# A list scheduler's DMA rate: 310 GB/s in place of 360 in the plan of a fused long-convolution and MLP kernel

## The chip, the cores and the metric

The kernel runs on one core of a Trainium2 chip. The metric is device microseconds for one execution. The kernel before takes 866.74 us, the median of three runs (866.11 to 869.25).

The core has five instruction streams that matter here: TensorE (matmuls; PE in the profile, its weight loads PEld), VectorE (DVE), ScalarE (ACT), GpSimd (POOL, here nearly only issuing accumulating transfers) and SyncE (SP, which only issues transfers). Each works through its own queue in program order and waits for the others on semaphores.

## The reference: what is computed

Two kinds of layers alternate on a sequence of 2048 rows of 640 channels, each behind a layer norm and with a residual: A gates the normed rows with a long causal convolution, B is an MLP with a hidden width of 1728. The weights and the operands of A are the same both times.

```python
def _A_ref(q, k, v, shift_k, ssm_k, ssm_D):
    ...  # k_shift: causal depthwise convolution of k with 4 taps
    kv = k_shift * v
    ...  # y: causal depthwise convolution of kv with ssm_k, 2048 taps, by FFT
    y = y + kv * ssm_D[None, None, :]
    return q * y

def _B_ref(x, w1, w2):
    h = jnp.maximum(jnp.einsum("bsd,df->bsf", x, w1), 0)
    return jnp.einsum("bsf,fd->bsd", h, w2)

x = A_q
x = x + _A_ref(_layernorm(x), A_k, A_v, A_shift_k, A_ssm_k, A_ssm_D)
x = x + _B_ref(_layernorm(x), B_w1, B_w2)
x = x + _A_ref(_layernorm(x), A_k, A_v, A_shift_k, A_ssm_k, A_ssm_D)
x = x + _B_ref(_layernorm(x), B_w1, B_w2)
```

## The kernel before

**Tiling.** The 2048 rows are cut into 8 chunks of 256, each of two halves of 128 rows; the 640 channels into 5 tiles of 128. The convolution does not depend on x, so its result (Y, kept in DRAM) is made once and used by both A layers. It is done chunk by chunk in a transformed domain: `transform` loads a unit (one or two tiles of a chunk: kt, vt, hf, hr), applies the four taps (ACT L381 and DVE L412 or L418, product with v at L419, sums at L421 and L422, filter sums gs at L403), and transforms signal and filter with matmuls against constant matrices (pg L435, L458; pt L481; pr L498; split in three matmuls at L315 to L317) into A and G tiles of 128x768 (results moved at L438, L462 to L464, L473, L508, L511). `spills` writes these to DRAM (L528, L529), and `products` reads them again for all later chunks (Ax, Gx at L566), multiplies and sums them on VectorE (L575, L578, L579), and transforms back (pq at L601 or L315 to L317, ys at L633 and L634, stored at L642).

**The MLP.** `norms` loads all weights (ws, L674), squares them on TensorE (pw, L681) for a scale (L686 to L697, pn at L688), and `wsplit` makes two half-precision parts of each (ScalarE L708, VectorE L709). `prep` makes the layer input of a chunk: norm, gate with Y, residual, norm (L765 to L786, L827, L831), and splits it in two half-precision parts (xh at ACT L860 and DVE L861; in the first chunk at L840 to L845). These are transposed by transposing transfers (L873) or, for the very first 128 rows, by TensorE (xt, L880, copied out at L884 and L886). `main` multiplies with w1 (h and hb, L994, L996, L1006, L1007, L1009), splits the activations into a high part hh (ScalarE, L1045) and a low part hl (VectorE, L1046), with special lines for the last narrow block (tb L1049, L1058, L1050, L1051, L1059, L1060), and multiplies with w2 (o and oc, L978, L979, L981). The residual goes in at L1136. The last three MLP layers take another form of the second product (L933).

**What sets the order.** All of this is recorded as operations of a `Plan`: engine, estimated cost, tiles read and written, priority, and for transfers the bytes. `Plan.order` runs a list schedule over a modelled clock: whenever an engine is free, it takes the ready operation of the best priority whose output tiles have room. The order found is then issued and fixed; on the chip no engine departs from it. Three places use the modelled transfer:

- An operation with `nbytes` set moves a variable `dma`, the time at which the modelled transfer path is free: it starts from the later of its old value and now plus 1.9 us, and grows by bytes over a rate. The tiles written become ready 1.1 us later (L201 to L204).
- SyncE takes nothing while `dma` lies more than `LAG` (3 us) ahead of now (the lines at the start of the loop over engines). In that time operations of better priority may become ready and go first.
- Everything that reads a loaded tile becomes ready after it, and so the order of TensorE, VectorE and ScalarE follows too.

Priorities (`CLS`): urgent steps of the MLP first, then loads for it (SOON), the convolution of the first chunks (CONV), spills (SPILL), the convolution of later chunks (LATER), and MLP matmuls as filler (FILL). Rings of buffers (`Ring`) bound how far work can run ahead: 4 buffers each for Ax and Gx together and for A and G, one each for kt, vt, hf, hr.

Of the kernel before, what the change touches and what calls it, by code (L numbers as in the profile page):

```python
# [45 lines left out]
CRIT, SLACK = -1, 0.6  # L46
PEOUT = 0.35
SAFE = 1.5
LATE_DOWN = 0.0


def LATE(o):
    return SAFE if o.prio[0] in CLS[3:5] else o.late

# [39 lines left out]
class Plan:  # L94
# [33 lines left out]
    def order(self):  # L128
        engs = sorted({o.eng for o in self.ops})
        free = dict.fromkeys(engs, 0.0)  # L130
        cand = {e: [] for e in engs}
        soon = {e: [o for o in self.ops if o.eng == e and o.prio[0] == CRIT] for e in engs if e != "SP"}
        for o in self.ops:
            if not o.left:
                cand[o.eng].append(o)
        events, dma, n, out = [0.0], 0.0, 0, []

        def fits(o):
            at = {}
            for t in o.new:  # L140
                k = at.setdefault(t.ring, {})
                if sum(k.values()) >= t.ring.free or t.ring.lines[t.stream][k.get(t.stream, 0)] is not t:
                    return False
                k[t.stream] = k.get(t.stream, 0) + 1
            return True

        finish, later = [], []
        now = 0.0
        while n < len(self.ops):
            if not events:  # L150
                stuck = [(o.eng, o.seq, [t.name for t in o.new]) for e in engs for o in cand[e]]
                raise RuntimeError(f"no order: {stuck[:12]}")
            now = heapq.heappop(events)
            while events and events[0] <= now:
                heapq.heappop(events)
            while finish and finish[0][0] <= now:
                _, _, o = heapq.heappop(finish)
                for t in o.tiles:
                    t.left -= 1
                    if not t.left and t.ring is not None:  # L160
                        t.ring.free += 1
                for d in o.outs:
                    if d.eng == "PE" != o.eng and LATE(d):
                        heapq.heappush(later, (now + LATE(d), d.seq, d))
                        heapq.heappush(events, now + LATE(d))
                        continue
                    if d.eng == "PE" == o.eng:
                        continue
                    d.left -= 1
                    if not d.left:  # L170
                        cand[d.eng].append(d)
            while later and later[0][0] <= now:
                _, _, d = heapq.heappop(later)
                d.left -= 1
                if not d.left:
                    cand["PE"].append(d)
            for e in engs:
                if free[e] > now + 1e-9:
                    continue
                if e == "SP" and dma > now + LAG:  # L180
                    heapq.heappush(events, dma - LAG)
                    continue
                best = None
                rooms = [(max(d.ready for d in o.deps) - now + SLACK, o.prio) for o in soon.get(e, ()) if o.left and all(d.start is not None for d in o.deps)]
                for o in cand[e]:
                    if best is not None and o.prio > best.prio:
                        continue
                    if any(o.cost > room and o.prio > prio for room, prio in rooms):
                        continue
                    if fits(o):  # L190
                        best = o
                if best is None:
                    continue
                cand[e].remove(best)
                for t in best.new:
                    t.ring.free -= 1
                    t.ring.lines[t.stream].pop(0)
                best.start = now
                free[e] = now + best.cost
                end = free[e] + (PEOUT if e == "PE" else 0.08)  # L200
                if best.nbytes:  # L201
                    dma = max(dma, now + 1.9) + best.nbytes / 360e3
                    end = dma + 1.1
                best.ready = end  # L204
                if best.prio[0] == CRIT and e in soon:
                    soon[e].remove(best)
                if e == "PE":
                    for d in best.outs:
                        if d.eng == e:
                            d.left -= 1  # L210
                            if not d.left:
                                cand[e].append(d)
                heapq.heappush(finish, (end, best.seq, best))
                heapq.heappush(events, end)
                heapq.heappush(events, free[e])
                out.append(best)
                n += 1
        return out, now
# [11 lines left out]
def tile_h3_mlp(ctx: ExitStack, tc: tile.TileContext, q, kT, vT, shk, hF, hR, dD, w1, w2, cM, cG, out):  # L230
# [21 lines left out]
    def pe(cost, fn, reads, writes, prio, late=0.0):  # L252
        plan.op("PE", cost, fn, reads, writes, prio, late=late)

    def act(n, fn, reads, writes, prio, extra=0.0):
        plan.op("ACT", 0.1 + n * 0.00083 + extra, fn, reads, writes, prio)
# [632 lines left out]
    def main(n, a, layer, S, xTS):  # L889
# [130 lines left out]
        for j in JS:  # L1020
# [36 lines left out]
            if j == NFP - 1:  # L1057
                pe(0.0545 * len(S), lambda p1=p1: PE.matmul(p1[:, 0:R], down.t, tb[:, 0:R], start=False, stop=True, skip_group_check=True), [tb, down], [p1], URGENT, LATE_DOWN * len(S) / 2)  # L1058
                act(R, lambda p1=p1, hh=hh: ACT.activation(hh[0:64, z], p1[0:64, 0:R], AF.Relu), [p1], [hh], URGENT)  # L1059
# [134 lines left out]
    for n, (a, l, S) in enumerate(order):  # L1194
        nxt = xTs[1] if n == 0 else xT
        if n + 1 < len(order):
            na, nl, nS = order[n + 1]
            if n == 0 or nl == 0 and nS == (1,):
                pass
            elif nl == 0:  # L1200
                conv_to(na)
                if WINO and (na, nl) == WINO[0]:
                    wcombine()
                nxt = prep(na, 0, both)
        main(n, a, l, S, xT)
        if n + 1 < len(order) and nl == 1:
            nxt = prep(na, 1, nS)
        xT = nxt
# [87 lines left out]
```

## Time and profile before

| | us |
|---|---|
| median of three runs | 866.74 (866.11 to 869.25) |
| the profiled execution | 871.61 |
| its span, first to last instruction | 869.6 |
| TensorE busy in the span | 844.5 |
| VectorE busy | 743.4 |
| ScalarE busy | 481.3 |
| granted TensorE clock, mean | 0.996 |
| bytes moved by DMA | 181.18 MB, 208 GB/s over the span |

How to read it: a row of a timeline has the start in us from the first instruction, the length, the engine, the line of the kernel, the operation, the tiles (written <- read, with buffer numbers left out), the shapes, and in brackets the idle time before it on its engine and what ended that. Matmuls overlap, so the length of one is longer than the step from one start to the next; the same holds, by less, for VectorE. A row of SyncE gives the issuing of a transfer, not the transfer itself.

### The profile page before, as it was taken

The page shows a single profiled execution, that of the slowest core. Times are in us where ns is not written, and L with a number is a line of the kernel's source. Part 1 is how long each engine was busy: PE and PEld are TensorE (multiplying, and loading weights), DVE is VectorE, ACT ScalarE, POOL GpSimd, SP SyncE. Part 2 cuts the span into 40 slices and gives each one's busy share as a digit, 9 for nine tenths or more (in the row PEclk, how much of TensorE's full clock was granted, in tenths as well). Part 3 has the DMA queues.
Part 4 walks back from the last instruction along what each step waited for, and adds up shares of the span by engine and source line. Part 5 has one row for each costly group of instructions (what it writes and reads, how often), then busy time and mean ns, then how long its engine had stood idle before and what let it go on. Part 6 is the DMA issues. An engine that isn't in the chain of part 4 may idle for free.

```text
span 869.6 us, 19562 instructions
## 1 busy us (share of the span) xinstructions
PE 844.5 (97%) x7738; PEld 661.3 (76%) x7738; DVE 743.4 (85%) x1367; ACT 481.3 (55%) x1121; POOL 46.3 (5%) x57
## 2 busy tenths in 40 slices
PE   8899999999989999999999999999999999999997
PEld 7767778778768777776777777777677777888886
DVE  7999999999889999989999999999888575646543
ACT  6697686437476385726548274644516365827331
POOL 1000000000010001101000010100000000000000
PEclk9999999999999999999999999999999999999999
DMA  9994867898999959898889797788896561110200
GB/s 329 391 308 141 259 213 254 243 341 259 309 220 316 343 159 260 217 223 215 221 226 267 192 260 173 219 230 249 231 310 220 144 202 32 37 26 1 33 29 31
DMA packets 134989, 181.18 MB, mean 208 GB/s; under 512 B 50673, under 2 KB 87281, under 8 KB 134898
## 3 DMA queue, kind: packets, MB, share of 16 engines
q1 hardware_dynamic: 126578, 169.46, 62.8%
q0 software_dynamic: 8320, 10.49, 7.8%
q8 instruction: 60, 0.98, 0.5%
q14 instruction: 31, 0.25, 0.1%
HBM read 123.61 MB, written 35.65 MB: 183 GB/s over the span
## 4 chain that ended last, share of the span: by engine, by line
PE 42%; DVE 36%; DMA 12%; issue 4%; ACT 4%; SPq 2%; DVEq 0%; POOL 0%; ACTq 0%
DVE pd L578 8%; DVE pacc L579 7%; PE o L933 6%; PE h L1006 6%; PE h L1007 6%; PE h L1009 6%; DMA Gx<-G 3%; PE o L978 3%; PE o L979 3%; PE o L981 3%; DVE hl L1046 2%; DVE pacc L575 2%; DVE acc L418 2%; DVE xh L861 1%; DMA kt<-in_kT 1%
## 5 line engine op out<-in xcount | busy, mean ns | idle before, releaser
L1007 PE MATMUL h<-xT,w 128*128 128x256 f16 (+1 forms) x1290 | 301.8, 252 | 2.8 <-DMA xT<-xh 2.8
L1006 PE MATMUL h<-xT,w 128*128 128x256 f16 (+1 forms) x1290 | 302.0, 252 | 1.0 <-DVE hl L1051 0.6
L1009 PE MATMUL h<-xT,w 128*128 128x256 f16 (+1 forms) x1290 | 301.9, 252 | 0.5 <-DVE w L709 0.5
L1007 PEld LDWEIGHTS <-w 128*128 128x128 f16 x1390 | 136.2, 98 | 12.9 <-issue 2.2
L1006 PEld LDWEIGHTS <-w 128*128 128x128 f16 x1390 | 136.1, 98 | 10.8 <-DMA xT<-xh 0.6
L978 PE MATMUL o<-w,hh 128*128 128x512 f16 x364 | 138.4, 380 | 1.8 <-DVE gt L464 1.2
L979 PE MATMUL o<-w,hh 128*128 128x512 f16 x364 | 138.2, 380 | 0.0
L1009 PEld LDWEIGHTS <-w 128*128 128x128 f16 x1290 | 126.4, 98 | 12.8 <-issue 3.1
L579 DVE TENSOR_TENSOR pacc<-pacc,pd 128x768 f32<-128x768 f32 x140 | 133.4, 953 | 0.7
L981 PE MATMUL o<-w,hl 128*128 128x512 f16 x338 | 128.4, 380 | 2.3 <-DVE negmA L762 1.2
L978 PEld LDWEIGHTS <-hh 128*128 128x128 f16 x728 | 71.4, 98 | 48.7 <-issue 2.4
L979 PEld LDWEIGHTS <-hh 128*128 128x128 f16 x728 | 71.4, 98 | 45.3 <-issue 0.3
L981 PEld LDWEIGHTS <-hl 128*128 128x128 f16 x676 | 66.2, 98 | 43.8 <-DVE hl L1046 2.5
L1045 ACT ACTIVATE hh<-h 128x512 f16<-128x512 f32 (+1 forms) x103 | 50.2, 487 | 86.2 <-PE h L1009 86.2
L578 DVE TENSOR_TENSOR pd<-Ax,Gx 128x768 f32<-128x768 f32 x87 | 81.9, 953 | 9.1 <-DMA Gx<-G 8.9
L978 PE MATMUL oc<-w,hh 128*128 128x128 f16 x364 | 79.8, 219 | 0.0
L979 PE MATMUL oc<-w,hh 128*128 128x128 f16 x364 | 79.8, 219 | 0.0
L981 PE MATMUL oc<-w,hl 128*128 128x128 f16 x338 | 74.1, 219 | 0.0
L1046 DVE SCALAR_TENSOR_TENSOR hl<-h,hh 128x512 f16<-128x512 f32 (+1 forms) x103 | 57.9, 562 | 12.1 <-ACT hh L1045 11.8
L381 ACT ACTIVATE tp<-kt,shs 128x256 f32<-128x256 f32 (+1 forms) x78 | 43.5, 575 | 23.2 <-DVE acc L418 13.1
L578 DVE TENSOR_TENSOR pd<-at,Gx 128x768 f32<-128x768 f32 x44 | 41.4, 954 | 1.7 <-DMA Gx<-G 1.4
L399 POOL DMA_DIRECT2D gs<-hr x20 | 18.4, 919 | 438.8 <-DMA vt<-in_vT 189.5
(225 smaller groups left out, 1557.2 us busy)
## 6 DMA issues: line engine op xcount, KB each, us to landing
Ax<-A SPq DMA_DIRECT2D x91, 384.0 KB, 4.6
Gx<-G SPq DMA_DIRECT2D x91, 384.0 KB, 4.5
G<-gt SPq DMA_DIRECT2D x32, 384.0 KB, 4.2
A<-at SPq DMA_DIRECT2D x32, 384.0 KB, 5.2
y<-Y SPq DMA_DIRECT2D x30, 320.0 KB, 4.4
ws<-in_w SPq DMA_DIRECT2D x28, 320.0 KB, 6.6
x<-in_q SPq DMA_DIRECT2D x16, 320.0 KB, 5.4
out_dram<-x SPq DMA_DIRECT2D x16, 320.0 KB, 3.6
```

The lines of the kernel that those rows point to most:

```text
L381: ACT.activation(o[:, i : i + m], kview(i, m, j), AF.Copy, scale=shs[:, t, j : j + 1])
L578: ew(f"mac{j % POOLMOD}", 768, lambda e, pd=pd, av=av, gv=gv: e.tensor_mul(pd.t, av(), gv()), [ax, gx], [pd], pr_)
L579: dve(768, lambda i=i, pd=pd: DVE.tensor_add(acc[:, i], acc[:, i], pd.t), [acc, pd], [acc], pr_)
L933: PE.matmul(b[:, c : c + w], x, y[:, z : z + w], start=done[i] == 1, stop=done[i] == total[i])
L978: PE.matmul(z, hh[:, c], wh[:, d], start=(j == JS[0] and i == 0 and (h == 0 or s == S[0])), stop=False)
L979: PE.matmul(z, hh[:, c], wl[:, d], start=False, stop=end and tail)
L981: PE.matmul(z, hl[:, c], wh[:, d], start=False, stop=end)
L1006: PE.matmul(p[:, z], wh, xv(t, 0), start=b, stop=False)
L1007: PE.matmul(p[:, z], wh, xv(t, 1), start=False, stop=tail and e)
L1009: PE.matmul(p[:, z], wl, xv(t, 0), start=False, stop=e)
L1045: act(2 * R, lambda p=p, hh=hh: ACT.activation(hh.t, p.t, AF.Relu), [p], [hh], URGENT)
L1046: dve(2 * R, lambda p=p, hh=hh, hl=hl: DVE.scalar_tensor_tensor(hl.t, p.t, 0.0, hh.t, op0=ALU.max, op1=ALU.subtract), [p, hh], [hl], URGENT)
```

## The change

Two constants are named, the fixed time before a transfer keeps its value of 1.9 us, and the rate is 310e3 bytes per us in place of 360e3. Only the modelled clock in `Plan.order` reads them. The operations recorded, their costs on the engines, their priorities and the buffers are the same.

```diff
@@ -46,6 +46,7 @@
 CRIT, SLACK = -1, 0.6
 PEOUT = 0.35
 SAFE = 1.5
+DBW, DLAT = 310e3, 1.9
 LATE_DOWN = 0.0
@@ -199,7 +200,7 @@
                 free[e] = now + best.cost
                 end = free[e] + (PEOUT if e == "PE" else 0.08)
                 if best.nbytes:
-                    dma = max(dma, now + 1.9) + best.nbytes / 360e3
+                    dma = max(dma, now + DLAT) + best.nbytes / DBW
                     end = dma + 1.1
                 best.ready = end
                 if best.prio[0] == CRIT and e in soon:
```

Line numbers in the text are those of the kernel before; in the changed kernel those behind line 48 are higher by one.

## The prediction

> **What bounds the kernel now.** I read the page first: the line of busy times, then the shares of the chain that ended last.
>
> ```profile
> span 869.6 us, 19562 instructions
> ...
> PE 844.5 (97%) x7738; PEld 661.3 (76%) x7738; DVE 743.4 (85%) x1367; ACT 481.3 (55%) x1121; POOL 46.3 (5%) x57
> ...
> PE 42%; DVE 36%; DMA 12%; issue 4%; ACT 4%; SPq 2%; DVEq 0%; POOL 0%; ACTq 0%
> ```
>
> TensorE is idle for 869.6 - 844.5 = 25.1 us of the span, yet the chain runs almost as much through VectorE as through TensorE. To see where each counts I asked for the busy time by stage (after the stage and its length: TensorE, its weight loads, VectorE, ScalarE, GpSimd; then the granted clock, the share of the DMA engines and GB/s).
>
> ```profile
> 0.00:50.00 50.00, 42.93 (x411) 38.12 (x412) 42.80 (x110) 33.47 (x75) 4.14 (x17) 0.97 0.99 355
> 50.00:75.00 25.00, 22.70 (x259) 16.96 (x258) 24.80 (x46) 21.54 (x40) 0.00 (x0) 1.00 0.60 198
> 75.00:250.00 175.00, 171.79 (x1891) 137.76 (x1889) 165.90 (x322) 109.41 (x275) 4.85 (x5) 1.00 0.84 261
> 250.00:275.00 25.00, 22.02 (x244) 16.94 (x242) 20.73 (x38) 17.60 (x46) 1.20 (x1) 0.93 1.22 303
> 275.00:330.00 55.00, 54.99 (x481) 42.44 (x480) 53.94 (x84) 28.84 (x67) 6.24 (x6) 1.00 0.81 246
> 330.00:640.00 310.00, 305.78 (x2520) 231.77 (x2520) 299.52 (x480) 166.84 (x388) 29.87 (x28) 1.00 0.86 230
> 640.00:870.00 230.00, 224.33 (x1948) 177.31 (x1945) 135.75 (x295) 103.55 (x235) 0.00 (x0) 1.00 0.30 89
> ```
>
> TensorE's idle time is 7.1 us up to 50, then 2.3, 3.2, 3.0, nothing, 4.2, and 5.7 in the last stage, after its last matmul. So TensorE's queue, in its fixed order, sets the time; VectorE, 24.8 of 25 us busy from 50 to 75, sets what TensorE waits for early on. An order of the same instructions can gain at most that idle time, and loses whatever new waits it makes.
>
> **The change part by part.** No instruction is added or removed. The planner's clock for DMA slows down, and so the fixed orders differ. I set the two programs' orders side by side: of TensorE's 14,600 rows 5,806 stand elsewhere, of VectorE's 1,299 there are 991, of ScalarE's 1,043 there are 712, of SyncE's 580 there are 347. In the last seventh of the run TensorE's and VectorE's orders are the same again.
>
> *Is the new figure nearer to the chip?* The planner lands a load at issue + 1.9 + bytes/rate + 1.1 us when nothing is queued. The page's part on DMA issues (KB each, median us to landing) and SyncE's timeline (start, length) say:
>
> ```profile
> Ax<-A SPq DMA_DIRECT2D x91, 384.0 KB, 4.6
> ...
> ws<-in_w SPq DMA_DIRECT2D x28, 320.0 KB, 6.6
> ```
>
> ```profile
> 12.23 18.85 SPq L674 DMA_DIRECT2D ws<-in_w  x25
> ```
>
> A 384 KB load (393,216 bytes) costs 4.09 us at 360 and 4.27 at 310; the trace has 4.6, so for a lone load the new figure is a little nearer. A stream says the opposite: 25 weight loads of 327,680 bytes issue in 18.85 us, which is 434 GB/s, and at 310 they would take 26.4 us. So the plan now believes that the weights, and with them the MLP, come several us later than they do. By the Trainium skill (DMA: Bandwidth & Descriptors, Where 436 GB/s comes from) a transfer from HBM is held to about 358 GB/s and only the on-chip side reaches 435, which would speak for the old 360 and against this change; this row lies at the higher number, and at 358 those loads would take 22.9 us. Neither number enters the sum.
>
> *The head, up to 50 us.* TensorE waits first for the weight loads, then for a norm factor, then for the first row block (xh); its timeline, with the idle time before a row in brackets, and one row of VectorE's:
>
> ```profile
> 37.37 0.46 PE L681 MATMUL pw<-ws 128*128 128x128 bf16 x5 [0.36 <-DMA ws<-in_w]
> 39.09 0.38 PE L688 MATMUL pn<-ws,ones 128*128 128x1 f32 x2 [1.26 <-DVE dg L686]
> 40.38 0.71 PE L880 MATMUL xt<-ident,xh 128*128 128x128 f16 x5 [0.91 <-ACT xh L844]
> ```
>
> ```profile
> 38.95 0.88 DVE L709 SCALAR_TENSOR_TENSOR w<-ws,wsc,w 128x640 f16<-128x640 f32 x1
> ```
>
> The new order puts the transposes L880 ahead of the last four groups of L681 and ahead of L688. They still wait for xh, whose chain on ScalarE is not shorter: two weight copies go behind its square sum, but one still stands between its root and L844. So the start of the MLP, right behind L880, stays, and four groups of at most 0.46 us, 1.8 us, leave a wait and partly enter the MLP. Their cover is the 2.3 us that TensorE idles from 50 to 75: nothing, or 1.8 if that cover goes; I take nothing. On VectorE the split at 38.95 now stands behind L845, which needs the same xh, so VectorE gets a hole of one split, some 0.8 us, and at 24.8 of 25 us busy it does not make it up: +0.8 on all that VectorE sets, or zero if other work fills it.
>
> *75 to 250 us.* Here the new order gives convolution work on VectorE precedence over the low halves of the MLP activations (hl, L1046). The clearest place, then the rows that price it, from VectorE's and TensorE's timelines:
>
> ```profile
> 145.29 0.42 DVE L1046 SCALAR_TENSOR_TENSOR hl<-h,hh 128x256 f16<-128x256 f32 x1
> ...
> 146.16 0.38 PE L981 MATMUL o<-w,hl 128*128 128x512 f16 x1
> ```
>
> ```profile
> 190.28 0.95 DVE L579 TENSOR_TENSOR pacc<-pacc,pd 128x768 f32<-128x768 f32 x1
> 191.15 0.69 DVE L403 TENSOR_TENSOR gs<-hf,hr 128x512 f32<-128x512 f32 x1
> 191.75 0.42 DVE L1046 SCALAR_TENSOR_TENSOR hl<-h,hh 128x256 f16<-128x256 f32 x1
> ```
>
> ```profile
> 192.10 0.28 PE L315 MATMUL pr<-sh,cMh 128*128 128x256 f32 x1
> 192.22 0.28 PE L316 MATMUL pr<-sl,cMh 128*128 128x256 f32 x1
> ```
>
> From start to start, a 128x768 product costs VectorE 191.15 - 190.28 = 0.87 us, a 128x512 one 0.60, and a split matmul TensorE 0.12. Ahead of the hl at 145.29 come three of the first, two of the second and two tiny ones: 3.8 us, and nothing leaves. Its matmul at 146.16 gets 12 split matmuls more ahead, 1.4 us, and had 146.16 - 145.71 = 0.45 us to spare: 3.8 - 1.4 - 0.45, some 2 us late. How much of it remains, the next tight place shows:
>
> ```profile
> 229.06 0.42 DVE L1046 SCALAR_TENSOR_TENSOR hl<-h,hh 128x256 f16<-128x256 f32 x1
> ...
> 229.54 0.39 PE L981 MATMUL o<-w,hl 128*128 128x512 f16 x1 [1.18 <-DVE negmA L762]
> ```
>
> This wait exists already (the release is put down to L762, but the hl ended 0.06 us before). VectorE gets four instructions of 0.60 more ahead (2.4 us), TensorE 16 matmuls of 0.12 (1.9): the end of the wait moves by 2.4 + 0.8 - 1.9 = 1.3 us against the work done. So the 2 us are not added to it; they are swallowed by this wait, down to +1.3.
>
> *250 us.* The largest wait of the run follows, for two transposing transfers (L873), the second of which carries what L861 writes.
>
> ```profile
> 244.16 0.82 DVE L861 TENSOR_TENSOR xh<-xnB,xh 128x640 f16<-128x640 f32 x1
> ```
>
> ```profile
> 252.68 0.23 PE L1006 MATMUL h<-xT,w 128*128 128x128 f16 x1 [0.40 <-DMA xT<-xh]
> 255.49 0.26 PE L1007 MATMUL h<-xT,w 128*128 128x128 f16 x1 [2.58 <-DMA xT<-xh]
> ```
>
> ```profile
> 398.03 0.39 PE L978 MATMUL o<-w,hh 128*128 128x512 f16 x1 [1.18 <-DVE gt L464]
> 398.26 0.38 PE L979 MATMUL o<-w,hh 128*128 128x512 f16 x1
> 399.52 0.39 PE L981 MATMUL o<-w,hl 128*128 128x512 f16 x1 [0.88 <-DVE hl L1046]
> ```
>
> Ahead of L861 six VectorE instructions are new: three of 0.60 and three of half that size or less, taken at 0.30, 2.7 us. Ahead of the matmul at 252.68 come 12 of the MLP, six at 398.26 - 398.03 = 0.23 and six of a quarter of the columns at 0.06: 1.7 us. With the hole: 2.7 + 0.8 - 1.7 = +1.8 us. If the transposes land faster than here, TensorE still carries the +1.3 from 229; if no TensorE work covers the shift, +3.5; if the shift is soaked up before it, zero. I take +1.8; the whole MLP of that block is queued behind this wait.
>
> *After 256 us.* VectorE's hl stand about 1 us of work earlier, the matmuls that use them at the same places. At the pair of waits at 398.03 and 399.52 one ScalarE instruction less stands ahead of the hh and three VectorE ones ahead of the hl: the two waits, 2.06 us, shrink or vanish. Against that stand waits which the reordered 310 us may make anew: bounded by zero and by the 4.2 us that TensorE idles there in the old order. I set these two off: 0, between -2.1 and +4.2.
>
> **Sum:** +1.8 us (lowest 0 - 2.1 = -2.1, highest 3.5 + 4.2 = +7.7), on the profiled execution's 871.6 us, which is its span of 869.6 and 2.0 around it. That execution is 4.9 us above the median of the runs, 866.74; I carry the difference over to the median: 868.5 us.
>
> **The rivals.**
>
> *Faster: the waits go.* The head's waits for weights and norm factor leave the queue, the transposes at 250 land early enough, and the waits at 398 vanish. For it: VectorE's hl are earlier after 256. Against it: in the head the wait for xh takes over, and L861 goes later, not earlier. Price: 0.40 + 2.58 + 2.06 = 5.0 us less: about 862 us.
>
> *Slower by much: SyncE's queue blocks.* With slower modelled DMA the planner holds loads back until transposes overtake them, and SyncE issues in order.
>
> ```profile
> 43.80 0.32 SPq L566 DMA_DIRECT2D Ax<-A  x1
> 44.22 0.38 SPq L566 DMA_DIRECT2D Gx<-G  x1
> 47.19 1.32 SPq L873 DMA_TRANSPOSE xT<-xh  x1
> ```
>
> This transpose, which waits for its xh, now stands ahead of four transfers, these two loads among them, which then issue after 47.19, some 4 us later. It decides where a held load has less than 4 us to spare, most easily near 250, where the DMA engines are at 1.22 of their share. Two such places at 4 us, and once more a stage at 0.93 of the clock (0.07 of 25 us, 1.75), make +9.8: about 877 us. Against it: the loads held in the head are used only after 70 us. The Trainium skill (TensorE: Matmul & The Clock Gate, Part 1) has idleness bring half the clock until the array has been busy for some 3.4 us; the 0.93 beside the longest wait agrees.
>
> *Nothing: the shifts are soaked up.* VectorE idles 9.1 us from 75 to 250 and ScalarE is 55% busy: 866.7 us. Against it: the margins at 146 and 229 are under half a us.
>
> **How the numbers follow.** Forecast as summed, 0.40; nothing, 0.11; faster, 0.20; slower by much, 0.29. A change within 0.5%, 862.4 to 871.1 us, cannot be told from none here. The forecast's own spread (864.6 to 874.4 by the bounds) leaves 0.29 of its 0.40 inside and 0.11 above; with the nothing case and 0.02 of the faster one 0.42 is inside. That gives faster 0.18, same 0.42, slower 0.40. The range is 861 to 879: it takes in the faster case's price and most of the blocked queue.
>
> **What would show it.** In the changed profile: the first MLP matmuls near 42 us and a gap of some 0.8 us on VectorE just before; waits for hl between 90 and 230 of some 2 us together; a wait of 3 to 4 us for the transpose near 255 to 258; the pair of waits near 400 under 1.3 us. Wrong, if TensorE's idle time after 330 us changes by over 3 us, or if VectorE waits for Gx or kt loads where it did not before.

## The result, and the profile after

The changed kernel takes 863.76 us, the median of 8 runs (862.84 to 864.79); the kernel before took 867.25 on the same chip (8 runs, 863.86 to 870.43). The ratio is 0.9957 with a 95% interval from 0.9936 to 0.9977: faster by 0.43%, where 868.5 us had been predicted. A ratio leaves out disturbed runs; of the kernels below only s2 has any, two of 879 us, without which its median is 872.0. The profiled execution took 864.42 us. That of the kernel before took 871.61, 4.4 us over its median, so that the two profiles differ by twice what the medians do. The page of the changed kernel, in the lines that were shown of the kernel before:

```profile
span 862.6 us, 19571 instructions
...
PE 843.1 (98%) x7738; PEld 662.2 (77%) x7738; DVE 744.0 (86%) x1367; ACT 483.2 (56%) x1121; POOL 46.4 (5%) x57
...
PE 66%; DVE 16%; ACT 7%; issue 5%; DMA 5%; SPq 1%; POOL 0%; DVEq 0%; POOLq 0%; ACTq 0%
```

All engines do the work that they did before. What changed is the chain that ended last: VectorE had 36% of it and transfers 12%, now 16% and 5%. The busy time by stage, in the same columns (stage and its length, TensorE, its weight loads, VectorE, ScalarE, GpSimd, granted clock, share of the DMA engines, GB/s):

```profile
0.00:50.00 50.00, 42.83 (x401) 39.13 (x402) 41.09 (x112) 30.55 (x69) 4.11 (x17) 0.93 0.87 319
50.00:75.00 25.00, 21.40 (x230) 15.51 (x230) 24.65 (x38) 23.09 (x44) 0.00 (x0) 1.00 0.80 267
75.00:250.00 175.00, 174.21 (x1931) 140.34 (x1929) 168.12 (x328) 111.92 (x279) 5.20 (x5) 1.00 0.88 267
250.00:275.00 25.00, 24.23 (x302) 18.82 (x299) 24.41 (x44) 16.38 (x45) 0.91 (x1) 1.00 1.02 282
275.00:330.00 55.00, 53.68 (x441) 41.16 (x439) 52.16 (x80) 31.36 (x71) 7.58 (x7) 1.00 0.91 248
330.00:640.00 310.00, 310.00 (x2562) 234.96 (x2561) 300.65 (x482) 165.93 (x384) 28.59 (x27) 1.00 0.85 231
```

TensorE's idle time by stage is 7.2, 3.6, 0.8, 0.8, 1.3 and 0 us, where it was 7.1, 2.3, 3.2, 3.0, 0 and 4.2. So the head got worse (by 1.4 us) and the stretch from 75 to 640 us better (by 7.5), all but the stage from 275 to 330, which lost 1.3. TensorE is busy in every one of the 310 us of the long middle stage. The grouped waits of TensorE name what went (who waited for whom, us in all, how often, the longest). Before:

```profile
PE h L1007 <- DMA xT<-xh: 2.8, 2, 2.6
PE hb L1058 <- ACT tb L1049: 2.1, 3, 1.5
...
PE hb L1006 <- DVE hl L1046: 1.2, 1, 1.2
PE o L978 <- DVE gt L464: 1.2, 1, 1.2
PE o L981 <- DVE negmA L762: 1.2, 1, 1.2
PE o L981 <- DVE hl L1046: 1.2, 2, 0.9
```

After:

```profile
PE xt L881 <- ACT xh L845: 3.5, 1, 3.5
PE hb L1059 <- ACT tb L1050: 2.2, 4, 1.0
...
PE o L980 <- DVE w L710: 1.4, 2, 0.8
PE h L1007 <- DVE hh L1061: 1.3, 1, 1.3
```

The waits for the transposes at 250 us, the one at 229 and the pair at 398 are gone, and so is one of 1.5 us for tb at 626.67. (The waits for tb are as large in all as before, but the longest is now 1.0 us, at 313.83.) In the head the wait for xh grew from 0.91 to 3.46 us, those for weight splits (w) from 0.5 to 2.3 in all, and the last row, 1.3 us, stands at 67.77. Not every wait of a profile belongs to its order: in c1 below, which has the order of before and leaves nothing out ahead of 238 us, the wait at 229 is missing and TensorE is there 1.85 us earlier.

The long wait at 255 us had a second price. The granted clock (the share of its full clock that TensorE was given) was 0.93 in that stage and is 1.00 now; 0.07 of 25 us is 1.75 us, of which c1 below shows 1.3 on the matmuls. Behind that wait the matmuls of 128 columns start 0.107 us apart, and only 0.056 apart in c1, which has no such wait.

In the table of runs below, TensorE's waits are counted more finely: the step from the start of one matmul to the start of the next, less the median step of matmuls of that kind (the same line and shape), summed. So the count holds also what a lower clock adds to a step. In the first 75 us this count is uncertain by about 1 us, since the clock granted there differs between profiles (0.93 to 1.00); there the start of a given matmul near 130 us, ahead of which every order compared there has the same matmuls, is the better measure, though the clock moves it too.

### The profile page after: what moved, and what is told of

Same layout as the page of the kernel before. It is cut to its first block, busy times and chain, and to the rows that moved or that the text cites. A ratio compares the mean times of both kernels' runs of the same rounds, so it can differ in the third digit from the quotient of the medians.

```text
span 862.6 us, 19571 instructions
## 1 busy us (share of the span) xinstructions
PE 843.1 (98%) x7738; PEld 662.2 (77%) x7738; DVE 744.0 (86%) x1367; ACT 483.2 (56%) x1121; POOL 46.4 (5%) x57
## 4 chain that ended last, share of the span: by engine, by line
PE 66%; DVE 16%; ACT 7%; issue 5%; DMA 5%; SPq 1%; POOL 0%; DVEq 0%; POOLq 0%; ACTq 0%
PE h L1007 10%; PE h L1010 10%; PE h L1008 10%; PE o L934 7%; PE o L979 6%; PE o L980 6%; PE o L982 6%; DVE pacc L580 2%; PE oc L980 2%; PE oc L979 2%; DVE pd L579 1%; PE oc L982 1%; DVE hl L1047 1%; DMA Ax<-A 1%; DVE pacc L576 1%
## 5 line engine op out<-in xcount | busy, mean ns | idle before, releaser
L1047 DVE SCALAR_TENSOR_TENSOR hl<-h,hh 128x512 f16<-128x512 f32 (+1 forms) x103 | 58.1, 564 | 14.8 <-ACT hh L1046 14.5
```

The costliest lines, as they stand in the source:

```text
L1047: dve(2 * R, lambda p=p, hh=hh, hl=hl: DVE.scalar_tensor_tensor(hl.t, p.t, 0.0, hh.t, op0=ALU.max, op1=ALU.subtract), [p, hh], [hl], URGENT)
```

## The experiments

Two questions: which part of the new order gains and which loses, and whether 310 is a better rate or only gave a good order.

| kernel | median, us (runs) | before beside it | ratio, 95% interval | TensorE's waits: to 75, 75-250, 250-350, 350-640 us |
|---|---|---|---|---|
| before (360) | 867.25 (8) | | | 10.0, 6.8, 5.7, 6.2 |
| changed (310) | 863.76 (8) | 867.25 | 0.9957 (0.9936-0.9977) | 12.7, 2.9, 3.2, 1.1 |
| s1 old head, new tail | 861.55 (8) | 868.38 | 0.9932 (0.9909-0.9955) | 8.9, 4.4, 2.5, 1.1 |
| s2 new head, old tail | 874.09 (12) | 868.38 | 1.0042 (1.0008-1.0076) | 12.5, 8.1, 6.3, 4.0 |
| s3 310 for SyncE's rule only | 871.81 (12) | 868.38 | 1.0043 (1.0019-1.0068) | 11.0, 6.8, 7.5, 4.4 |
| s4 310 for ready times only | 882.97 (6) | 868.38 | 1.0176 (1.0141-1.0212) | 13.0, 13.4, 9.2, 8.6 |
| c1 before without 3 accumulates | 865.42 (6) | 868.78 | 0.9975 (0.9946-1.0004) | 9.1, 5.8, 1.1, 8.0 |
| 250 GB/s | 934.80 (4) | 868.78 | 1.0773 (1.0737-1.0809) | 14.5, 13.1, 7.6, 31.4 |
| 300 GB/s | 871.79 (10) | 868.10 | 1.0041 (1.0019-1.0063) | 13.9, 4.3, 7.1, 5.6 |
| 320 GB/s | 867.90 (10) | 868.10 | 0.9994 (0.9971-1.0017) | 12.8, 6.6, 2.7, 2.6 |
| 335 GB/s | 869.94 (4) | 868.78 | 1.0028 (0.9993-1.0063) | 10.8, 4.2, 2.6, 7.8 |
| 434 GB/s | 888.63 (4) | 868.78 | 1.0244 (1.0207-1.0280) | 15.2, 9.6, 8.2, 8.4 |
| e1 310 to 100 us, then 360 | 873.55 (7) | 868.10 | 1.0078 (1.0044-1.0112) | 12.8, 7.1, 3.1, 5.8 |
| e2 360 to 100 us, then 310 | 864.70 (10) | 866.98 | 0.9965 (0.9944-0.9987) | 9.4, 5.7, 1.2, 3.3 |

### Which part of the order gains: splices

```diff
+    def spliced(self, T, first, second):
...
+        a, _ = self.order(first)
+        head = [o for o in a if o.start < T]
+        self.reset()
+        b, _ = self.order(second)
...
+        seen = set(head)
+        seq = head + [o for o in b if o not in seen]
+        return self.order(second, {e: [o for o in seq if o.eng == e] for e in {o.eng for o in seq}})
...
-        out, end = self.order()
+        out, end = self.spliced(75.0, 360e3, DBW)
```

s1 takes what the plan at 360 starts before 75 us of the plan's own clock in that plan's order, and all the rest in the order of the plan at 310; s2 calls it with the two rates exchanged. The order is then handed out queue by queue, with no choice left.

> The order of the kernel before (rate 360) for every operation that the plan starts before 75 us, then the remaining operations in the order of the changed kernel (rate 310). In the changed kernel's profile TensorE had waited 4.7 us more than before by 100 us, and 4.7, 2.6 and 1.6 us of waits near 398, 255 and 627 us had gone. Theory 1, the gain is made by the order after 75 us and the head loses: this beats both, about 860 us (2 to 5 us under the changed kernel), with the waits near 255 and 398 gone and no loss by 100 us. Rival 2, the late head itself makes the later waits vanish, since TensorE then arrives later: about the time before, 866 to 868 us, with the waits near 255 and 398 back. Rival 3, any reordering scatters by some 3 us: no pattern, and the waits that vanish are others.

> The mirror image: the changed kernel's order (rate 310) for what the plan starts before 75 us, then the order of before. Theory 1: the loss of the head without the gain of the tail, 870 to 872 us, slower than before by 3 to 5 us, and the waits near 255 and 398 are there. Rival 2: TensorE arrives 3 to 5 us later, so the later waits shrink as in the changed kernel, 864 to 866 us. Rival 3: anything from 862 to 872, with waits elsewhere.

s1 beats both kernels (the changed one by 1.4 us beside it on one chip, see below) and s2 is slower than both: the tail gains, the head loses. In s2 TensorE comes to the matmul that stood at 229.54 us only at 233.08, and yet the transposes are waited for again; rival 2, by which lateness itself dissolves the waits, falls. Of the pair at 398 only the second is back, 0.89 us. TensorE's timeline in s2:

```profile
257.12 0.23 PE L1032 MATMUL h<-xT,w 128*128 128x128 f16 x1 [0.89 <-DMA xT<-xh]
259.46 0.22 PE L1033 MATMUL h<-xT,w 128*128 128x128 f16 x1 [2.11 <-DMA xT<-xh]
```

The splices show a second difference, in VectorE's waits for loads. This is the view of one line's instructions (the loads of Ax and Gx) that are issued between 75 and 330 us: who waited for them (us, times), and the time to landing. Before:

```profile
who waited for it (us, times):
  DVE pd L578: 2.7, 3
...
DMA to landing us min/median/max: 2.9/5.3/7.3
```

After, with nobody in the list:

```profile
who waited for it (us, times):
busy tenths in 40 slices 0000000000000000000000000000000000000000
DMA to landing us min/median/max: 3.0/4.8/7.4
```

In s1 again nobody waits; in s2 VectorE waits 3.5 us, three times. The plan at 310 expects every load later; that it therefore lets VectorE take other work first, so that the load has landed when its turn comes, fits this but is argued. Counted over all loads whose first reader runs between 75 and 330 us, 13 were read within 0.3 us of landing in the kernel before, 2 in the changed one, 3 in s1, 14 in s2. A like count in the second profiles gives 3 for the changed kernel and 6 for s1, so a difference of 3 says nothing.

### The other end of the wait at 250 us: c1

```diff
-lambda g=g: POOL.dma_start(out=g.t, in_=hr.t, accum_op=ALU.add)
+lambda g=g, few=nm == "4_1": POOL.dma_start(out=g[:, :, 0:2] if few else g.t, in_=hr[:, :, 0:2] if few else hr.t, accum_op=ALU.add)
...
-lambda: POOL.dma_start(out=x[:, :, 2], in_=x[:, :, 1], accum_op=ALU.add)
+lambda few=nm == "4_0" and x is gt: POOL.dma_start(out=x[:, 0, 2, 0, 0:2] if few else x[:, :, 2], in_=x[:, 0, 1, 0, 0:2] if few else x[:, :, 1], accum_op=ALU.add)
```

> The kernel before with its order unchanged, but three accumulating transfers of GpSimd that issue at 240.46, 241.72 and 246.38 us beside the two transposes at 243.77 move two columns or less instead of 256 KB each (the sums that they make are left out). In the kernel before these transposes take 4.46 us to issue and land after 8.9 and 9.6 us; in the two kernels with the new tail no accumulating transfer stands beside them, they take 2.7 us to issue and land after 5.7 to 6.7, and TensorE's wait of 3.3 us is gone. Theory, the accumulating transfers hold the transposes up: landing after 5 to 7 us, the wait near 252 to 255 under 0.8 us, total 2 to 3 us less, 865 to 866 us. Rival, the plain loads in front of them (four of 384 KB and 256 KB from 240.1 to 243.2) do it: landing still after 8 to 9.5 us, the wait near 3 us, total as before, 867 to 868 us.

The kernel c1 leaves nearly all of three sums out; its order is that of before. GpSimd's timeline of the kernel before, with the three transfers; then the two transposes, first in SyncE's timeline, then by their time to landing:

```profile
240.46 0.86 POOL L399 DMA_DIRECT2D gs<-hr  x1 [24.78 <-ACT varB L776]
241.72 1.20 POOL L467 DMA_DIRECT2D gt<-gt  x1 [0.40 <-ACT hh L1050]
246.38 0.91 POOL L399 DMA_DIRECT2D gs<-hr  x1 [3.45 <-ACT hr L398]
```

```profile
243.77 4.46 SPq L873 DMA_TRANSPOSE xT<-xh  x2
```

```profile
DMA to landing us min/median/max: 8.9/9.2/9.6
```

In c1, with the same loads in front of them and the same order:

```profile
242.88 2.62 SPq L873 DMA_TRANSPOSE xT<-xh  x2
```

```profile
DMA to landing us min/median/max: 6.1/6.5/6.9
```

The two landed after 8.9 and 9.6 us, now after 6.9 and 6.1, and TensorE's waits of 0.40 and 2.58 us are gone: the accumulating transfers did it, not the loads. The stage has its full clock again, as its row of busy times shows (0.93 before):

```profile
250.00:275.00 25.00, 24.57 (x283) 19.24 (x282) 24.64 (x43) 17.96 (x45) 3.29 (x3) 1.00 1.08 329
```

TensorE is 0.9 us earlier than in the kernel before at 240 us and 5.5 us earlier at 258: of the 4.6 between, 3.0 are the two waits and 1.3 the faster steps behind them. The time of the whole is 0.25% less by the ratio, whose interval just reaches 1, and 3.4 us by the medians: less than those 4.6, and not clear of the noise. The new order escapes the same collision without leaving anything out. Its GpSimd transfers stand at 231.85, 234.63 and 247.32 us, its transposes at 244.56, and these land after 5.7 and 6.7. The Trainium skill (DMA: Bandwidth & Descriptors, Issuing engines are not separate DMA queues) has transfers run on the same 16 engines and interleave, whichever engine started them; c1 agrees, with 3.0 us of waits as the price here; which part of the path the transfers share is not shown.

The pair of waits near 398 us is still there in c1, only 5.4 us earlier with all the rest: nothing in it hangs on the transposes at 250. Behind it the clock is lower in c1 (0.89 from 385 to 400 us, 1.00 in the kernel before), and of the 5.4 us some 3.7 are left at 401.

### A better rate, or one good order

> The rate 310 only in the rule by which SyncE holds loads back (the modelled path more than 3 us ahead); the times at which loaded tiles count as ready stay at 360. If what matters is which loads SyncE lets through and when, this gives most of the change, 863 to 865 us, with the head's loss of 3 to 5 us too. If what matters is when loads count as ready, and so TensorE's and VectorE's order, it is near 867 us. If it is chance, neither: anything from 860 to 872.

> The mirror image: 310 only in the time at which loaded tiles count as ready, SyncE's rule at 360. If the order of TensorE and VectorE follows from the ready times and the gain from it, 863 to 865 us; if SyncE's rule carries the gain, near 867 us; if it is chance, anything from 860 to 872, with the remaining waits of TensorE at other places than in either kernel.

> The changed kernel with the rate 250 GB/s. In the profile of before the 384 KB loads that are used between 75 and 330 us land after 4.95 to 5.4 us on average, where the plan has 4.1 us at 360 and 4.3 at 310, so both rates are too fast there. Theory, the slower rate is nearer to the chip and its order has fewer waits for loads: at 250 (4.6 us) the same or better, 858 to 864 us. Rival, each rate is another draw from orders that scatter: no trend, 862 to 880 us. Either way the head loses more, 3 to 6 us by 100 us, since the weights' modelled stream is 1.7 times slower than the 434 GB/s measured.

> The changed kernel with 300 GB/s. Theory, the region around 310 is the better rate: 862 to 866 us. Rival, the order at 310 is one lucky draw: anything from 862 to 885 us, with waits of 2 us and more at places where 310 has none.

> The changed kernel with 320 GB/s. Theory of the better rate: 862 to 866 us. Rival, a draw: anything from 862 to 885 us.

> The changed kernel with the rate 335 GB/s, half way back. Theory of a better rate: between the two, 863 to 867 us. Rival, a draw: anything from 862 to 880 us, outside of the two as easily as between them.

> The changed kernel with the rate 434 GB/s, the rate at which the weight loads issue at the start. Theory of a better rate after 75 us: late loads become more frequent, slower than before, 869 to 875 us, though the head is as good as before's (no more than 7.5 us of TensorE waits by 56 us). Rival, a draw: anything from 862 to 880 us.

```diff
-DBW, DLAT = 310e3, 1.9
+DBW, DLAT = 300e3, 1.9
```

In s3 a second variable is kept for SyncE's rule; s4 has the two rates exchanged:

```diff
-if e == "SP" and dma > now + LAG:
-    heapq.heappush(events, dma - LAG)
+if e == "SP" and gate > now + LAG:
+    heapq.heappush(events, gate - LAG)
...
-dma = max(dma, now + DLAT) + best.nbytes / DBW
+dma = max(dma, now + DLAT) + best.nbytes / 360e3
+gate = max(gate, now + DLAT) + best.nbytes / DBW
```

Each half of the change alone is slower than no change; what was expected of the halves fell, and s4 (883 us) lies even outside the bounds that were set for chance. So does 250 GB/s (935 us), whose head is 4.5 us worse as expected, and 434, whose head was expected to be as good as before's and has 15.2 us of waits against 10.0. The neighbours 300 and 320 are slower or equal, 335 equal or slower, and the far ends cost 2.4 and 7.7%. If 310 were nearer to the chip and that were the reason, 300 or 320 would show it (862 to 866 expected). Nor do loads that are read as they land decide the time: the slowest order, at 250, has none between 75 and 330 us, and the order at 300 has few (3) and still loses, by waits of another kind: 2.83 us for a transpose and 3.32 us for a low half of the activations (hl). Two rows of its TensorE timeline:

```profile
271.75 0.26 PE L1007 MATMUL hb<-xT,w 128*128 128x128 f16 x1 [3.32 <-DVE hl L1047]
...
495.82 0.31 PE L1007 MATMUL h<-xT,w 128*128 128x256 f16 x1 [2.83 <-DMA xT<-xh]
```

> The plan runs on 360 GB/s up to 100 us of its clock and on 310 after. Up to 120 us its orders are those of the kernel before; after that they are neither those of the kernel before nor those of the changed kernel, since the plan goes on from another state. Theory, 310 is the better rate for the part after 75 us: 860 to 864 us, with fewer than five loads used within 0.3 us of landing between 75 and 330 us (before 13, changed 2). Rival, the gain of the new tail is the draw of one order: anything from 862 to 880 us, as for 335, 250 and 434 GB/s.

> The mirror image of the last switch: the plan runs on 310 GB/s up to 100 us of its clock and on 360 after. Theory, 310 is worse in the head and 360 worse after it: both losses, 869 to 873 us, with ten or more loads used within 0.3 us of landing between 75 and 330 us. Rival, a draw: anything from 862 to 885 us.

```diff
-dma = max(dma, now + DLAT) + best.nbytes / DBW
+dma = max(dma, now + DLAT) + best.nbytes / (DBW if now >= 100.0 else 360e3)
```

e2, whose tail is a third order, came out at 864.7, 0.35% under before, 0.7 us above the range that the better rate was given, with 7 late loads where fewer than five were expected; e1, its mirror image, lost 0.8%, with 11. Both have the sign that the theory of a better rate gives. But five rates between 300 and 360 give 871.8, 863.8, 867.9, 869.9 and 867 to 869 us with no trend, and so 310 is read as one good draw. That a slower rate for the tail alone does better on average rests on e2 and s1, two orders; it stays open.

### What the head loses

Four kernels are the changed one with a few instructions of the head put back, in a fixed order, and nothing else moved. Of hA and of hW the lines that move them (`put` moves operations ahead of another, or behind it); hP moves the groups alone, to the same place, and hAP moves them and hA's copies:

```diff
+        early = [o for o in seq if o.eng == "ACT" and any(t.name.startswith("ws") for t in o.tiles)]
+        at = seq.index(next(o for o in seq if o.eng == "ACT" and any(t.name.startswith("xl0_0") for t in o.tiles)))
+        early = [o for o in early if seq.index(o) > at][:2]
+        seq = [o for o in seq[:at]] + early + [o for o in seq[at:] if o not in early]
```

```diff
+        xt, xl = find("PE", "xt0_0_00"), find("DVE", "xl0_0_00", "xh0_0_00")
+        groups = [o for o in seq if o.eng == "PE" and any(t.name == "pw1" for t in o.tiles) and seq.index(o) > seq.index(xt)]
+        put(groups, xt)
+        put([find("PE", "pn1")], xt, True)
+        put([find("DVE", "dg1")], xl)
+        put([find("DVE", "wn21", "pn1")], xl, True)
+        put([find("ACT", "wnr1", "wn21")], find("ACT", "xT0_0_00"), True)
+        put([find("DVE", "wpw1", "wnr1"), find("DVE", "wsc1", "wpw1")], find("DVE", "xT0_0_01"), True)
```

> The changed kernel with one thing of the head put back: on ScalarE the first two weight copies (L709) stand ahead of the square sum of xh (L841) again, as in the kernel before, where ScalarE otherwise idles 2.06 us. Nothing else moves. In the changed kernel TensorE waits 0.48, 0.77, 0.80 and 0.91 us for weight splits between 48.9 and 58.2 us (before: 0.68 in all there), and 3.6 us for xh at 35.5. Theory, the late weight copies make the loss of 50 to 75 us: those waits shrink by 1.5 to 2.3 us, and the time by the same, 861.5 to 862.5 us. Rival, the squaring groups that were moved into the MLP make it: no gain, 863 to 864.5 us.

> The changed kernel with the other thing of the head put back: on TensorE the last four squaring groups (L682) stand ahead of the first transposes (L881) again, so that they run in the wait for xh. Nothing else moves. Theory, four groups of 0.53 us leave the MLP: TensorE's wait for xh shrinks from 3.6 to about 1.5 us, but the weight splits are then no earlier against an MLP that runs 2.1 us ahead, so their waits grow by up to 2.1 us: gain between 0 and 1 us, 862.8 to 864 us. Rival, the groups alone cost 2 us: 861.7 us.

> Both of these put back together. Theory: head as good as in the kernel before or nearly so, the gains add up, 860 to 862 us, and no kernel here is faster by more than 1 us. Rival, the loss lies in the rest of the reordered head (VectorE's order, loads): 863 to 864.5 us.

> The changed kernel with the whole chain of the second weight matrix's scale put back: on TensorE the four squaring groups ahead of the first transposes, and the norm matmul (L689) right behind them; on VectorE and ScalarE the five small instructions between it and the scale (L687, L690, L691, L692, L693) next to the places that they have in the kernel before. Theory, this chain makes the loss of the head: the scale is ready near 42 us instead of 48.3, the weight splits of the second matrix come 2 to 3 us earlier, TensorE's waits of 0.48, 0.77, 0.80 and 0.91 us between 48.9 and 58.2 shrink to 0.7 in all, and the time is that of the spliced kernel with the old head, 861 to 862 us. Rival, VectorE's order in the head makes it: waits as with the groups alone, 862.5 to 863.5 us.

> The kernel with the old head and the new tail once more, beside the changed kernel on one chip. If the head's loss of 3 to 4.7 us by 100 us lasts, it is 1.5 to 4 us under the changed kernel; if it is soaked up later, the two are within 1 us.

> The changed kernel itself, on the same chip as the spliced one: 863 to 865 us, 1.5 to 4 us over the spliced one if the head's loss lasts.

| kernel | median, us (runs) | ratio to before | the same matmul starts at, us |
|---|---|---|---|
| changed | 863.76 (8), again 863.87 (12) | 0.9957, 0.9976 (0.9954-0.9997) | 132.16, again 131.40 |
| hA copies put back | 863.40 (12) | 0.9959 (0.9937-0.9981) | 131.23 |
| hP groups put back | 862.91 (12) | 0.9952 (0.9935-0.9969) | 130.12 |
| hAP both | 862.52 (12) | 0.9941 (0.9923-0.9960) | 129.62 |
| hW groups and scale chain | 862.55 (10) | 0.9937 (0.9915-0.9960) | 129.80 |
| s1 whole old head | 861.55 (8), again 862.50 (12) | 0.9932, 0.9955 (0.9933-0.9977) | 129.65, again 129.80 |

The last column reads like this, in the changed kernel, in hAP and in s1 (TensorE's timeline):

```profile
132.16 0.38 PE L982 MATMUL o<-w,hl 128*128 128x512 f16 x1
```

```profile
129.62 0.38 PE L1011 MATMUL o<-w,hl 128*128 128x512 f16 x1
```

```profile
129.65 0.38 PE L1007 MATMUL o<-w,hl 128*128 128x512 f16 x1
```

The changed kernel is there at 131.8 us (mean of two that lie 0.8 apart), s1 at 129.7: the head loses 2.1 us. With the four groups put back (hP) 1.7 of it is recovered. Among the profiles in which the granted clock up to 50 us was 0.97 (the changed kernel's second, hP, the first of s1) the loss is 1.75 and 1.3 of it come back. The rest is not explained: hAP and hW make it up, but in their profiles that clock was 1.00. The rows of hP and hAP:

```profile
0.00:50.00 50.00, 42.53 (x413) 37.56 (x414) 43.07 (x115) 32.26 (x72) 4.30 (x17) 0.97 0.88 319
0.00:50.00 50.00, 42.60 (x414) 37.13 (x414) 43.50 (x115) 33.17 (x72) 4.29 (x17) 1.00 0.89 321
```

The times alone do not part the four from the changed kernel: their intervals overlap its two. By the medians hA gains no more than its rival allowed, hP lies at the low end of its theory, and hAP and hW stay half a us above theirs. The reason for the loss is seen at the first transposes. After, with one of the four groups as it stands in the MLP, and in hAP:

```profile
39.19 0.71 PE L881 MATMUL xt<-ident,xh 128*128 128x128 f16 x5 [3.46 <-ACT xh L845]
...
42.89 0.74 PE L682 MATMUL pw<-ws 128*128 128x128 bf16 x5
43.43 0.31 PE L995 MATMUL h<-xT,w 128*128 128x128 f16 x1
```

```profile
38.73 0.46 PE L711 MATMUL pw<-ws 128*128 128x128 bf16 x5 [0.37 <-DMA ws<-in_w]
39.03 0.44 PE L910 MATMUL xt<-ident,xh 128*128 128x128 f16 x5
```

In the new order TensorE stands idle for 3.46 us and does the squaring afterwards, within the MLP; put back, it squares while it waits. A group takes 0.54 us there and 0.30 in hAP, at the full clock. All four at 0.54 are 2.1 us, of the 2.5 that this profile is behind (132.16 against 129.7). In the second profile of the changed kernel and in hA two of the four ran at the full clock: 1.6 us in all, with 1.7 and 1.5 lost.

The theory of the weight splits failed twice, in hA and in hW. The waits for them stayed. In hA:

```profile
48.52 0.38 PE L1004 MATMUL o<-w,hh 128*128 128x512 f16 x1 [0.31 <-ACT w L734]
49.51 0.38 PE L1005 MATMUL o<-w,hh 128*128 128x512 f16 x1 [0.61 <-DVE w L735]
52.00 0.23 PE L1035 MATMUL h<-xT,w 128*128 128x128 f16 x1 [0.63 <-DVE w L735]
58.49 0.38 PE L1005 MATMUL o<-w,hh 128*128 128x512 f16 x1 [0.76 <-DVE w L735]
```

In hW, where the scale is made at 41.84 us instead of 48.19, three of them are left with 0.87, 0.71 and 0.67, all put down to VectorE's splits. TensorE comes to them earlier, and so waits as long as before. Over hP the earlier scale gains 0.3 us at that matmul, too little to tell from the clock. On one chip s1 is 1.4 us under the changed kernel by the medians, of 12 runs each (862.50 and 863.87; 860.87 to 864.60 and 861.32 to 866.10). That lies between what was expected of a loss that lasts (1.5 to 4) and of one that is soaked up (under 1); whether part of the 2.1 us is soaked up on the way cannot be told at this size.

## Why the prediction was wrong, point by point

Its direction was wrong, 868.5 us against 863.8, and its rival "faster: the waits go" (862) came true, to which it gave 0.20.

*The step that failed.* The only term of the sum other than zero was the wait at 250 us, +1.8, and instead the wait vanished: 3.0 us less, and with it the slow clock behind it, another 1.3. The transposes landed after 5.7 and 6.7 us, no longer 8.9 and 9.6, and the sum had held that landing fixed; c1 shows that accumulating transfers beside them had made it so long. Ahead of it VectorE's waits had been held fixed as well. The points in order:

*The bound.* Right: the time went by TensorE's idle time, and the work was the same. In the two profiles TensorE's idle time up to 640 us fell by 6.1 us and the span by 7.0.

*The new figure against the chip.* Rightly left out of the sum, though it was asked of the wrong row. The stream was also misread: 434 GB/s counts 25 loads over the 24 steps of their issue. From row to row they land 0.83 us apart, which is some 395 GB/s, still above both figures of the plan; and the 4.6 us is a median of 91 loads, not a lone one. What VectorE uses between 75 and 330 us lands after a median of 5.3 us (4.8 after), where the plan has 4.1 at 360 and 4.3 at 310. By the Trainium skill (DMA: Bandwidth & Descriptors, Anatomy of one DMA) a load of 384 KB comes, as an estimate, to 2.0 + 393,216/436,000 = 2.9 us, by a fit to transfers of GpSimd's. The fastest of these loads take just that, 2.9 and 3.0, the median 1.9 to 2.4 more. That points to waiting behind other transfers and not to the rate, which is argued and not tested.

*The head.* The mechanism was seen and the price was wrong. The start of the MLP near 42 us came (41.30), and so did a VectorE gap (0.56 us against 0.8). But the four groups, priced at 1.8 us by their length and then at nothing because TensorE idles 2.3 us between 50 and 75 us, cost their full 2.1 us in that profile, at its low clock. That idle time is spent on waits for other things; work put ahead of it does not fill it unless what is waited for stays where it is. Here that was late as well: the idle time from 50 to 75 us grew to 3.6.

*75 to 250 us.* This step failed first: "Ahead of the hl at 145.29 come three of the first, two of the second and two tiny ones: 3.8 us, and nothing leaves." The instructions were counted rightly, and VectorE's waits were held fixed. Two of them left, 1.47 us at 141.40 and 1.33 us at 81.4 (for ScalarE). VectorE's timeline before, and a row of its grouped waits:

```profile
141.40 0.83 DVE L827 TENSOR_TENSOR xnA<-y,xnA 128x640 f32<-128x640 f32 x1 [1.47 <-DMA y<-Y]
```

```profile
DVE at L511 <- ACT at L508: 1.3, 1, 1.3
```

In s1, which has the old head, the hl and its matmul stand at:

```profile
146.24 0.42 DVE L1072 SCALAR_TENSOR_TENSOR hl<-h,hh 128x256 f16<-128x256 f32 x1
```

```profile
148.27 0.38 PE L1007 MATMUL o<-w,hl 128*128 128x512 f16 x1
```

The hl is 0.95 us later than before (145.29), not 3.8, and its matmul 2.1 later (146.16), so that its margin grew. From 75 us to this hl VectorE waited 4.0 us in the kernel before and 1.3 in s1. The waits for hl of 2 us together between 90 and 230 us did not come: in the changed kernel TensorE waits 0.2 us there in all. VectorE was busy 168.12 us of the 175 instead of 165.90; it did 2.2 us more work in the stage.

*250 us.* Wrong in sign: +1.8 predicted, and the wait of 3 us gone. The transposes issue at 244.56 instead of 243.77, later by less than the head's loss alone, and the wait had been read as one for xh alone. c1 shows that 2.0 and 3.4 us of the two landings came from GpSimd's accumulating transfers beside them, and the sum had no term for those: it moved xh and its transposes, and kept the landing of 9 us. Nor had it one for the clock, 0.93 in that stage, which it used for a rival alone.

*After 256 us.* "I set these two off: 0" was a guess between -2.1 and +4.2 and came out past its lower end. The pair at 398 is gone as forecast (by the reason given or not, no run here shows), and the reordered stretch made no new waits (4.2 us of idle time to 0). The rest of the 4.2 was mostly the wait of 1.46 us for tb at 626.67, which the prediction does not list. From 275 to 330 us, where it saw nothing, 1.3 us of waits are new, 0.95 of them for tb at 313.83. Of the orders tried, the six with the changed kernel's tail have 1.1 to 1.5 us of waits there, and all others 2.6 or more. So waits anew were the rule, and this order the exception. Why it is one stays open.

*SyncE's queue blocks*, the rival at 877 with 0.29: no such stop is in the trace of the changed kernel, in which no instruction of VectorE waits for an Ax or Gx load from 75 to 330 us. Over the whole run VectorE waits 3.8 us for Gx, where it was 10.3. In s4 (883) it is 12.2, and TensorE waits 3.5 us for transposes and 11 for late hl; whether a blocked queue is behind that is open.

What would have shown it wrong was named: TensorE's idle time after 330 us changing by over 3. It did, by 4.2 up to 640 us (0.6 came back later).

## What to carry to other kernels

Where two engines both run near 100%, a reordering cannot be priced by counting what is put ahead of an instruction: list the waits of the other engine on the way, and the transfers in flight beside it, and ask which of them end sooner or later. A planner's constant is judged by the orders it gives, over several neighbouring values, not by its nearness to the chip; here one part in thirty moves the time by 0.4 to 0.8% (320 and 300 against 310, by the ratios), and the good part of one order can be spliced to the good part of another (862 us). Work that runs while an engine waits is free only there: moved behind the wait it costs its full length, here at a low clock besides.

## What the runs showed of the hardware

Three accumulating transfers of 256 KB from GpSimd's queue, issued from 3.3 us before to 2.6 us after two transposes, stretched the issue of the two from 2.62 to 4.46 us and their landing from 6.1 and 6.9 us to 8.9 and 9.6. Over all profiles but c1's, the transposes whose landing the profile tells landed after 3.6 us on average when none was in flight at their issue (845 of them), with one after 5.5 (103), with two or more after 6.3 (79). Other traffic differs between these places too; c1 alone holds it fixed.

The granted clock was 0.83 from 250 to 260 us in the kernel before, beside the wait of 2.58 us, and 1.00 there in c1 and in the changed kernel. Before, matmuls of 128 columns then started 0.107 us apart, in c1 0.056.

The kernel before scatters more than the changed one, though only the order differs: on one chip from 860.91 to 871.79 us in 23 runs, the changed one from 861.32 to 866.10 in 12. Its wait behind that collision is one candidate, but c1 without it still ran from 864.05 to 868.45. The waits at 222.75 and 229.54 us that its profile has and c1's has not are another, and so is the clock, which falls behind some of these waits. The cause is open.
